# Three stages on one core: the dense stage's first steps dealt out anew over the last attention periods, and later transfers regrouped

## The chip, the cores and the metric

One core of a Trainium2 chip runs the whole program. The metric is the device time in microseconds (us) of one execution. Engines by the names of the profile: PE is TensorE (matmuls and transposes), DVE is VectorE, ACT is ScalarE, POOL is GpSimd, SP is SyncE, which issues nearly all transfers (SPq is its sequencer).

## The reference

Talking-heads attention with B = 4, 12 heads, 448 positions, 64 values a head; then a dense layer 768 to 2048 to 768 with ELU; then a mixture of 8 experts, each token going to its best one, with a skip.

```python
scores = scale * q @ k.T
scores = einsum('bhij,hg->bgij', scores, w_pre)
attn = softmax(scores)
attn = einsum('bhij,hg->bgij', attn, w_post)
x = (attn @ v)                       # 1792 tokens of 768
h = x @ w_in                         # w_in, w_out come as float64
x = where(h > 0, h, exp(min(h, 0)) - 1) @ w_out
do_compute = x @ w_skip > 0
e_idx = argmax(xc @ w_gate)          # of the tokens with do_compute
h = maximum(xc[mask] @ w1[e], 0)     # for each expert e
out = x;  out[do_compute] = xc + prob * (h @ w2[e])
```

## The kernel before, in words

**Attention.** The queries are cut into 16 tiles (4 per batch, 120, 120, 120 and 88 queries), each into 3 units: NP = 48 periods. Period n runs the softmax of unit n and the second mixing and value product of units before it, and the scores of a tile five periods ahead. `relayout` (line 189) copies a unit's scores from the tile s into the eight buffers d by DMA, in a layout in which heads and queries share partitions (d<-s on SP, line 197); `mix_pre` (L205) multiplies them by the first mixing matrix, `top` (L213, DVE) takes the maxima, `softmax` (L226, ACT) the exponentials with their sums, `mix_post` (L265) the second mixing; its results are copied to `at` (L271, ACT and DVE) and `av` (L286, L293) multiplies them with v; DVE copies the product to x (L302, L305), and SP stores it to xT (L313). Each unit has two halves; the copies d of unit n + 1's second half and of unit n + 2's first half are issued in period n.

**Dense layer.** `mixtures` is a generator called mix; each `next(mix)` runs it to its next yield. In the last five periods (n = 43 to 47, the flag `late`) four steps are woven into each: after the softmax, after the copies, after the second `mix_post` and at the period's end. Two more follow while attention ends. The steps load a weight chunk f of float64 (L518), narrow it to float32 on the chip (L529 on ACT; L532, L534, L537 and L539 on DVE; L541 on POOL; a generator with steps of its own), and load blocks of tokens xr from xT (`load_x`, L552). `high_x` (L556, ACT) and `low_x` (L560, DVE) split each into a high and a low half, as is done for weights (`split`, L504 and L505), and a product is made of three matmuls (high x high, high x low, low x high). products(s) (L626) makes 18 matmuls for one weight chunk and one block of 448 tokens; `elu` (L633, L634, L636) follows. `w_jobs` narrows the following chunks. `tables` (L589 and around) loads the gate's weights wgt and transposes them. The order of everything up to `order.close()`, in `mixtures` behind `tables`, is the order of the code, because `manual_schedule` is open; from there a scheduler orders the instructions of each engine.

**Second dense product, routing and experts.** The second product (L899) goes over 14 tiles of 128 tokens. Its weights w_out are partly in memory already; seven narrowed chunks wf are loaded again (wr, L845) through the pool raw0 of three buffers. `route` and `seat` find a token's expert and place. The experts' stage gathers the tokens of each expert with an indirect DMA on POOL (xg, L1072), transposes them (pt, L1082), and multiplies by w1 (L1094) and w2 (L1107), whose low halves DVE makes (wlo, L1067). After the first two experts `plan` orders the rest, and `reorder` (L1030 to L1038) makes the index list `ordered` with six DVE operations, which the fourth gather needs.

All of SP's transfers go out in the order of its row; a transfer waits for the one eight before it.

Of the kernel before, what the change touches and what calls it, by code (L numbers as in the profile page):

```python
# [20 lines left out]
NK = DM // 128  # L21
# [57 lines left out]
def attention(tc, q, k, v, w_pre, w_post, xT, mix):  # L79
# [12 lines left out]
    with ExitStack() as ctx, ExitStack() as mixing, ExitStack() as scoring:  # L92
# [137 lines left out]
        def softmax(U):  # L230
            for e in exps(U):
                e()
# [160 lines left out]
        for n in range(NP):  # L393
# [34 lines left out]
            for U in cur[1:]:  # L428
                softmax(U)
            if late:  # L430
                next(mix)
            for m in moves:
                m[1](nc.scalar.copy)
                m[0](nc.vector.tensor_copy)
            keys = T1 < len(tiles) and tiles[T1][1] == 0
# [31 lines left out]
        moves[0]()  # L467
        moves.append(av(len(tiles) - 1, 2))
        for f in moves[1:]:
            f()  # L470
        store()
# [4 lines left out]
def mixtures(tc, order, xT, w_in, w_out, w_skip, w_gate, w1, w2, ident, gT, wf, wg, x2d, slots, out):  # L476
# [5 lines left out]
    with ExitStack() as top:  # L482
# [27 lines left out]
        with ExitStack() as ctx:  # L510
# [57 lines left out]
            def load_w_in(fc):  # L568
                return load_w(w_in[fc])
# [4 lines left out]
            def tables():  # L574
# [8 lines left out]
                nc.sync.dma_start(out=wgt[:, :, :E], in_=w_gate.rearrange("(k p) e -> p k e", p=128))  # L583
                nc.sync.dma_start(out=wgt[:, :, E], in_=w_skip.rearrange("(k p) -> p k", p=128))
# [59 lines left out]
            yield  # L644
            yield
# [3 lines left out]
            load_x(0)  # L649
            yield  # L650
            next(step)
# [5 lines left out]
            yield  # L657
            high_x(0, 0)
            yield
            low_x(0, 0)  # L660
            w = wi[0] = ring_a.tile([128, 2, DM], FP32R, tag="w", name="w")
            nc.scalar.copy(out=w[:, 0], in_=narrowed[0])
            yield
            nc.vector.tensor_tensor(out=w[:, 1], in0=narrowed.pop(0), in1=w[:, 0], op=ALU.subtract)
            high_x(0, 1)
            yield
            raws[1] = load_w_in(1)
            yield
            low_x(0, 1)
# [3 lines left out]
            high_x(0, 3)  # L673
            yield
            low_x(0, 3)
            yield
            load_x(1, range(4))
            yield
            high_x(0, 4)
# [22 lines left out]
            yield  # L702

# [5 lines left out]
            products(1)  # L709
            split_x(2, range(6))  # L710
            elu(1)
            load_x(3)
            products(2)
# [31 lines left out]
        with ExitStack() as ctx:  # L745
# [47 lines left out]
            def route(i, lg):  # L793
# [3 lines left out]
                nc.vector.max_index(out=ix, in_max=mx, in_values=lg[:, :E])  # L797
                nmx = st_p.tile([128, 1], FP32, tag="nmx", name="nmx")
# [6 lines left out]
                ef = st_p.tile([128, 1], FP32, tag="ef", name="ef")  # L805
                nc.vector.tensor_copy(out=ef, in_=ix[:, 0:1])
                do = st_p.tile([128, 1], FP32, tag="do", name="do")
                nc.vector.tensor_scalar(out=do, in0=lg[:, E:E + 1], scalar1=0.0, scalar2=None, op0=ALU.is_gt)
                oh = st_p.tile([128, E], FP32, tag="oh", name="oh")
                nc.vector.tensor_scalar(out=oh, in0=iota8, scalar1=ef, scalar2=do, op0=ALU.is_equal, op1=ALU.mult)  # L810
# [32 lines left out]
            for fc in range(EARLY, NF):  # L843
                raw = raw0.tile([128, 2 * DM], FP32, tag="w", name="wr")[:, :DM]
                last_wr = nc.sync.dma_start(out=raw, in_=wf[fc - EARLY])  # L845
                wo[fc] = split(raw, ring_a if fc < RA + RB else ring2)
# [41 lines left out]
            for i, n, fc, cs in work:  # L888
# [35 lines left out]
                if fc == NF - 1:  # L924
                    if 0 in cs:
                        x2 = rows[i] = x2_p.tile([128, DM], FP32, tag="x2", name="x2")
                    for c in cs:
                        to, at = x2[:, cols[c]], po[c][:, :cols[c].stop - cols[c].start]
                        nc.scalar.copy(out=to, in_=at)  # L929
                        if last and c == 1:  # L930
                            turned, freed = score_turned(x2, c)
                            place_old(range(2))
                            logits(turned)
                            place_old(range(2, 5))
# [5 lines left out]
            place_old(range(5, NK))  # L940
# [9 lines left out]
        with ExitStack() as ctx:  # L950
# [289 lines left out]
            expert_first([0], [h], jobs(((3, 2), turn_h, h, ht, 0)))  # L1240
            expert_second(0, ht, jobs(((0,), turn_h, h, ht, 1), ((2,), turn_x, 1)))
            h = new_h()
            expert_first([1], [h], jobs(((1, 2), turn_x, 2)))
            reorder()
            xg[3] = gather(ids[3])
# [111 lines left out]
```

## Time and profile before

| what | us |
|---|---|
| median of three runs | 1022.62 |
| their range | 1020.44 to 1026.99 |
| the profiled execution's own time | 1024.68 |
| its span, first to last instruction | 1022.9 |
| attention, to the end of its last value product | 0 to 362.38 |
| the woven periods, n = 43 to 47 | 311.49 to 348.66 |
| first dense product | 362.38 to 596.46 |
| second dense product and routing | 596.46 to 848.91 |
| experts' products | 848.91 to 1015 |

The profile is one execution. Its table of stretches gives each engine's busy time in a stretch, and the granted clock of TensorE as a share of full speed: 0.50 is 1.2 GHz, 1.00 is 2.4 GHz. The list of waits gives, for a line of one engine, what ended its idle time, the sum, the count and the longest. In the timelines a row starts with its start and its length; "<-" in the brackets names what ended the idle time ahead of the row.

### The profile page before, as it was taken

How to read it: one execution, taken by the hardware profiler on the slowest of the kernel's cores; microseconds unless marked ns; L12 is line 12 of the kernel's file. 1: busy time of each engine (PE TensorE's matmuls, PEld its weight loads, DVE VectorE, ACT ScalarE, POOL GpSimd, SP SyncE). 2: the span in 40 equal slices, each digit the busy share in tenths (PEclk: the TensorE clock that was granted, in tenths of full speed). 3: DMA queues.
4: the chain of work that ended last, by engine and by line, in shares of the span. 5: the costliest groups of instructions: out<-in, count | busy, mean ns of one | idle time of the engine just before them, and what ended most of it. 6: DMA issues, size and time to landing. Idle time of an engine off the chain costs nothing. (4 is left out here: it accounts for less than half of the span.)

```text
span 1022.9 us, 30007 instructions
## 1 busy us (share of the span) xinstructions
PE 982.5 (96%) x12226; PEld 860.5 (84%) x12226; DVE 725.8 (71%) x1458; ACT 555.9 (54%) x1121; POOL 226.8 (22%) x295
## 2 busy tenths in 40 slices
PE   7899999999998899999999999999999999899997
PEld 4577777777766788999999999999999988799987
DVE  5677776777765777666666477777777748999963
ACT  5687787788765654445444462222222116788851
POOL 2233224224223312232332200010101003321002
PEclk9999999999998989999999999999999999999999
DMA  4665665675646565454665489543434396999800
GB/s 157 214 206 158 218 208 149 205 235 131 216 167 204 160 220 166 156 183 151 227 220 192 140 281 301 155 124 93 123 95 123 99 344 237 393 396 398 322 9 34
DMA packets 132297, 199.67 MB, mean 195 GB/s; under 512 B 35476, under 2 KB 99480, under 8 KB 131901
## 3 DMA queue, kind: packets, MB, share of 16 engines
q1 hardware_dynamic: 130013, 191.27, 56.4%
q0 software_dynamic: 2144, 6.46, 1.6%
q8 instruction: 97, 1.59, 0.7%
q14 instruction: 43, 0.35, 0.1%
HBM read 122.47 MB, written 37.65 MB: 157 GB/s over the span
## 5 line engine op out<-in xcount | busy, mean ns | idle before, releaser
L899 PE MATMUL o<-w,gh 128*128 128x384 f32 (+2 forms) x1344 | 239.2, 337 | 1.2 <-DVE w L505 0.8
L899 PEld LDWEIGHTS o<-w,gh 128*128 128x128 f32 x1344 | 231.9, 188 | 4.5 <-DVE w L505 1.4
L626 PE MATMUL h<-xh,w 128*128 128x448 f32 x1152 | 235.4, 367 | 0.0
L626 PEld LDWEIGHTS h<-xh,w 128*128 128x128 f32 x1152 | 217.4, 189 | 17.3 <-issue 0.4
L265 PEld LDWEIGHTS f<-kr,e 64*64 64x64 f32 x5888 | 106.3, 136 | 39.1 <-issue 29.5
L213 DVE TENSOR_REDUCE nmx<-c 128x1 f32<-128x448 f32 x184 | 102.4, 617 | 51.7 <-PE c L205 51.6
L226 ACT ACTIVATE e<-c,nmx 128x448 f32<-128x448 f32 x184 | 114.2, 632 | 23.0 <-DVE nmx L213 22.8
L789 DVE SCALAR_TENSOR_TENSOR junk<-x,wrow 128x768 f32<-128x768 f32 x117 | 111.8, 955 | 18.3 <-ACT x L929 12.8
L246 POOL TENSOR_SCALAR kr<-kpost,rs 128x60 f32<-128x60 f32 x184 | 78.4, 448 | 200.1 <-DVE rs L241 110.2
L1067 DVE TENSOR_TENSOR wlo<-w1t,whi 128x1536 fp32r<-128x1536 f32 x64 | 111.0, 1751 | 14.3 <-ACT whi L1065 14.0
L265 PE MATMUL f<-kr,e 64*64 64x60 f32 (+1 forms) x5888 | 108.4, 219 | 7.3 <-issue 3.5
L541 POOL TENSOR_TENSOR wf<-a,p 128x768 f32<-128x768 f32 x32 | 66.6, 2081 | 187.2 <-DVE p L539 139.5
L1065 ACT CAST whi<-w1t 128x1536 fp32r<-128x1536 f32 x64 | 93.9, 1482 | 20.6 <-PE ph L1094 9.4
L164 PE MATMUL qk<-k,qq 64*120 64x448 f32 (+1 forms) x576 | 82.6, 408 | 8.1 <-ACT k L135 4.5
L774 ACT CAST gh<-gr 128x512 fp32r<-128x512 f32 x56 | 35.0, 624 | 98.7 <-PE o L899 39.1
L205 PE MATMUL c<-d,kpre_low 64*64 64x448 f32 x368 | 83.3, 554 | 3.0 <-ACT s L168 2.8
L205 PE MATMUL c<-d,kpre_up 60*64 60x448 f32 x368 | 81.8, 554 | 0.0
L271 ACT COPY at<-f 128x420 f32<-128x420 f32 (+1 forms) x136 | 65.4, 516 | 28.2 <-PE f L265 27.2
L164 PEld LDWEIGHTS qk<-k,qq 64*120 64x120 f32 (+1 forms) x576 | 52.1, 186 | 27.8 <-issue 4.6
L286 PE MATMUL xp<-at,v 128*64 128x120 f32 (+1 forms) x1152 | 67.5, 266 | 7.3 <-issue 3.9
L168 ACT ACTIVATE s<-qk 120x448 f32<-120x448 f32 (+1 forms) x96 | 51.7, 544 | 35.5 <-PE qk L164 26.4
L169 DVE TENSOR_SCALAR s<-qk 120x448 f32<-120x448 f32 (+1 forms) x96 | 58.3, 621 | 16.1 <-PE qk L164 8.4
(180 smaller groups left out, 1255.7 us busy)
## 6 DMA issues: line engine op xcount, KB each, us to landing
w1t<-in_moe_w_dram SPq DMA_DIRECT2D x64, 768.0 KB
d<-s SPq DMA_DIRECT2D x176, 210.0 KB
gT<-g SPq DMA_DIRECT2D x64, 224.0 KB
f<-in_moe_w_in_dram SPq DMA_DIRECT2D x16, 768.0 KB
f<-in_moe_w_out_dram SPq DMA_DIRECT2D x16, 768.0 KB
gr<-gT SPq DMA_DIRECT2D x48, 256.0 KB
rk<-in_k_dram SPq DMA_DIRECT2D x24, 224.0 KB
v<-in_v_dram SPq DMA_DIRECT2D x24, 224.0 KB
```

The lines of the kernel that those rows point to most:

```text
L164: nc.tensor.matmul(out=ps[:n, :S], lhsT=qt[T, p // 2][rows, a, p % 2, :n], rhs=kt[b, p][rows, z, :], start=(i == 0), stop=(i == 2))
L205: nc.tensor.matmul(out=ps[j * UP:(j + 1) * UP, :S], lhsT=kpre_up[UP:UP + HP, :] if z else kpre_low, rhs=d[z, j])
L213: nc.vector.tensor_reduce(out=t, in_=c, op=ALU.max, axis=AX.X, negate=True)
L226: nc.scalar.activation(out=e, in_=c, func=ACTF.Exp, bias=t, accum_out=sms[0][:, k + i:k + i + 1])
L246: nc.gpsimd.tensor_scalar(out=kr, in0=kposts[z], scalar1=rs[:, 2 * i + z:2 * i + z + 1], scalar2=None, op0=ALU.mult)
L265: nc.tensor.matmul(out=ps[to, heads, z, :], lhsT=e[rows, keys * JW:(keys + 1) * JW], rhs=kr[rows, first * HR:(first + n) * HR])
L286: nc.tensor.matmul(out=ps[i][z * 64:(z + 1) * 64, :n], lhsT=vt[b, p][:, jc * 2 + z, :], rhs=att[T][:, jc * H + ORDER.index(2 * p + z), :n] ...
L626: nc.tensor.matmul(out=ps, lhsT=w[:, a, kk, :], rhs=xs[tb, kk][:, z, :], start=(kk == 0 and a + z == 0), stop=(kk == NK - 1 and a == 1))
L789: nc.vector.scalar_tensor_tensor(out=t[:, o:o + n], in0=x2, scalar=1.0, in1=w, op0=ALU.mult, op1=ALU.mult, accum_out=lg[:, e:e + 1])
L899: mm = nc.tensor.matmul(out=po[c][:, :cols[c].stop - cols[c].start], lhsT=gs[i][fc // GC][:, a, fc % GC, :], rhs=wo[fc][:, z, cols[c]], st ...
L1065: nc.scalar.copy(out=hi, in_=t)
L1067: nc.vector.tensor_tensor(out=lo, in0=t, in1=hi, op=ALU.subtract)
```

## The change

It does six things. (A) In late periods the copies to `at` of the first `mix_post` now stand ahead of the second half's softmax, and the first woven step behind both. The steps themselves are dealt out anew: the first token block is loaded in three pieces (2, 2, 2) and from one step before the narrowing on; the narrowing begins one step later; chunk 1 and the second block's loads come at other steps. (B) products(1) moves to a step of its own between the second and third value product of attention's end. (C) The loads of wgt move from `tables` to just behind the loads of the fourth token block. (D) Two chunks wf share one buffer of raw0. (E) `reorder` and the fourth gather move ahead of the first expert's second product. (F) In `route` three small operations move ahead of the exponential; in the last tile one block of `place_old` moves to a place after the last route.

```diff
-            for U in cur[1:]:
-                softmax(U)
-            if late:
-                next(mix)
+            if not late:
+                for U in cur[1:]:
+                    softmax(U)
             for m in moves:
                 m[1](nc.scalar.copy)
                 m[0](nc.vector.tensor_copy)
+            if late:
+                for U in cur[1:]:
+                    softmax(U)
+                next(mix)
...
         moves = [av(len(tiles) - 1, 0), av(len(tiles) - 1, 1, [ps_f.tile([128, 512], FP32, tag="f", name="xp") for _ in range(2)])]
-        moves[0]()
-        moves.append(av(len(tiles) - 1, 2))
-        for f in moves[1:]:
+        for f in moves:
             f()
+        next(mix)
+        av(len(tiles) - 1, 2)()
         store()
...
-                nc.sync.dma_start(out=wgt[:, :, :E], in_=w_gate.rearrange("(k p) e -> p k e", p=128))
-                nc.sync.dma_start(out=wgt[:, :, E], in_=w_skip.rearrange("(k p) -> p k", p=128))
...
             raws[0] = load_w_in(0)
             yield
             yield
+            load_x(0, range(2))
+            yield
+            yield
+            load_x(0, range(2, 4))
             yield
             step = narrowing(raws.pop(0))
             next(step)
             yield
-            load_x(0)
-            yield
             next(step)
             yield
+            load_x(0, range(4, 6))
+            yield
+            high_x(0, 0)
+            yield
             next(step)
             yield
             narrowed[0] = next(step)
             yield
-            yield
-            high_x(0, 0)
+            raws[1] = load_w_in(1)
             yield
...
-            load_x(1, range(4))
-            yield
-            high_x(0, 4)
             yield
             low_x(0, 4)
...
             elu(0)
             wi[1] = split(narrowed.pop(1), ring_a)
             yield
+            products(1)
+            yield
...
             raws["out"] = load_w_out(0)
-            products(1)
             split_x(2, range(6))
             elu(1)
             load_x(3)
+            nc.sync.dma_start(out=wgt[:, :, :E], in_=w_gate.rearrange("(k p) e -> p k e", p=128))
+            nc.sync.dma_start(out=wgt[:, :, E], in_=w_skip.rearrange("(k p) -> p k", p=128))
             products(2)
...
-            for fc in range(EARLY, NF):
-                raw = raw0.tile([128, 2 * DM], FP32, tag="w", name="wr")[:, :DM]
-                last_wr = nc.sync.dma_start(out=raw, in_=wf[fc - EARLY])
-                wo[fc] = split(raw, ring_a if fc < RA + RB else ring2)
+            for f0 in range(EARLY, NF, 2):
+                raw = raw0.tile([128, 2, DM], FP32, tag="w", name="wr")
+                fcs = range(f0, min(f0 + 2, NF))
+                for fc in fcs:
+                    last_wr = nc.sync.dma_start(out=raw[:, fc - f0], in_=wf[fc - EARLY])
+                for fc in fcs:
+                    wo[fc] = split(raw[:, fc - f0], ring_a if fc < RA + RB else ring2)
...
-                            place_old(range(2, 5))
+                            place_old(range(2, 4))
...
-            place_old(range(5, NK))
+            place_old(range(4, NK))
...
             expert_first([0], [h], jobs(((3, 2), turn_h, h, ht, 0)))
+            reorder()
+            xg[3] = gather(ids[3])
             expert_second(0, ht, jobs(((0,), turn_h, h, ht, 1), ((2,), turn_x, 1)))
             h = new_h()
             expert_first([1], [h], jobs(((1, 2), turn_x, 2)))
-            reorder()
-            xg[3] = gather(ids[3])
```

ACT's row in the woven periods n = 43 to 45: at is the copy behind the second mixing, e an exponential with its sum, a the narrowing's first step on the weight chunk f. Before:

```order
L271 COPY at<-f 128x42x10 x2
L226 ACTIVATE e,sm<-c,nmx 128x448 x4
L271 COPY at<-f 128x42x10 x3
L529 ACTIVATE a<-f_7170 128x768
L226 ACTIVATE e,sm<-c,nmx 128x448 x4
L271 COPY at<-f 128x42x10 x3
```

and now:

```order
L271 COPY at<-f 128x42x10 x2
L226 ACTIVATE e,sm<-c,nmx 128x448 x2
L271 COPY at<-f 128x42x10
L226 ACTIVATE e,sm<-c,nmx 128x448 x2
L532 ACTIVATE a<-f_7172 128x768
L271 COPY at<-f 128x42x10 x2
```

The step on f stood ahead of period 44's exponentials and now stands behind them; a copy to at stands between the two pairs.

SP's row in the same periods: f is the weight chunk, d<-s a half unit's scores (two rows for each half), xT a stored value product, xr a load of 128 x 448 tokens. Before:

```order
L518 DMA f_7170<-in_moe_w_in_dram 128x1536
L197 DMA d_154<-s 120x1x448
L197 DMA d_155<-s 120x1x448
L313 DMA xT_60<-x 128x2x120
L197 DMA d_156<-s 120x1x448
L197 DMA d_157<-s 120x1x448
L552 DMA xr<-xT_57 128x448 x6
L197 DMA d_158<-s 120x1x448
L197 DMA d_159<-s 120x1x448
```

and now:

```order
L521 DMA f_7172<-in_moe_w_in_dram 128x1536
L555 DMA xr<-xT_57 128x448 x2
L197 DMA d_154<-s 120x1x448
L197 DMA d_155<-s 120x1x448
L313 DMA xT_60<-x 128x2x120
L197 DMA d_156<-s 120x1x448
L197 DMA d_157<-s 120x1x448
L555 DMA xr<-xT_57 128x448 x4
L197 DMA d_158<-s 120x1x448
L197 DMA d_159<-s 120x1x448
```

Two of the six loads xr moved ahead of the second half of unit 45 (d_154, d_155); the other four stay between unit 46's first half and its second.

PE's row at the end of attention: xp are the value products (three pieces of the last tile), h the products of the first dense layer, 18 matmuls for each products(s). Before:

```order
L286 MATMUL xp<-at,v 64x88 x12
L293 MATMUL xp<-at,v 64x88 x4
L286 MATMUL xp<-at,v 64x88 x12
L293 MATMUL xp<-at,v 64x88 x4
L626 MATMUL h<-xh,w 128x448 x175
L589 MATMUL pt<-ident,wgt 8x128 x6
```

and now:

```order
L627 MATMUL h<-xh,w 128x448 x18
L286 MATMUL xp<-at,v 64x88 x12
L293 MATMUL xp<-at,v 64x88 x4
L627 MATMUL h<-xh,w 128x448 x108
L590 MATMUL pt<-ident,wgt 8x128 x6
```

products(1) stands ahead of the third value product, and the transposes of wgt come after 108 more matmuls instead of 175.

## Rows read from the trace of the kernel before

**Rows 1.** The page's busy time of TensorE, its share and instructions.

```profile
PE 982.5 (96%) x12226; PEld 860.5 (84%) x12226; DVE 725.8 (71%) x1458; ACT 555.9 (54%) x1121; POOL 226.8 (22%) x295
```

**Rows 2.** Stretches: length, busy time of each engine, clock, DMA share, GB/s.

```profile
317.32:328.12 10.80, 6.59 (x188) 5.16 (x181) 5.69 (x12) 4.80 (x12) 2.06 (x5) 0.85 0.83 259
328.12:335.15 7.03, 7.03 (x192) 5.48 (x187) 4.28 (x10) 5.09 (x13) 4.02 (x6) 0.75 0.51 145
335.15:341.01 5.86, 5.33 (x186) 4.22 (x181) 5.58 (x13) 5.40 (x15) 2.75 (x5) 1.00 0.53 167
...
357.01:362.38 5.37, 2.46 (x33) 2.07 (x32) 2.99 (x7) 4.38 (x9) 0.00 (x0) 0.69 0.93 288
...
402.35:596.46 194.11, 194.11 (x963) 180.17 (x960) 124.50 (x180) 92.59 (x152) 53.26 (x26) 1.00 0.54 182
...
848.91:886.72 37.81, 37.55 (x191) 32.33 (x190) 37.54 (x71) 29.90 (x32) 15.46 (x11) 1.00 0.92 337
...
889.73:1015.00 125.27, 125.27 (x685) 115.67 (x686) 100.04 (x88) 83.03 (x82) 19.46 (x11) 1.00 0.66 253
```

**Rows 3.** TensorE's waits: line, releaser, us in total, times, longest.

```profile
PE pt L1082 <- DMA xg<-x2d,ordered: 3.0, 1, 3.0
PE xp L286 <- DVE x L302: 2.9, 1, 2.9
...
PE pt L589 <- DMA wgt<-in_moe_w_gate_dram: 2.2, 1, 2.2
PE f L265 <- DVE at L271: 2.1, 1, 2.1
...
PE o L899 <- DVE w L505: 0.8, 2, 0.4
...
PE o L899 <- ACT w L504: 0.4, 2, 0.2
```

**Rows 4.** Timelines of ACT and VectorE in period 44.

```profile
321.44 0.89 ACT L529 ACTIVATE a<-f 128x768 f32<-128x768 f32 x1 [2.92 <-issue]
...
322.36 0.56 DVE L532 TENSOR_SCALAR a<-a 128x768 int32<-128x768 int32 x1 [5.72 <-ACT a L529]
```

**Rows 5.** SP's timeline from 314; then transfers of 312 to 332, 40 slices.

```profile
314.46 1.67 SPq L518 DMA_DIRECT2D f<-in_moe_w_in_dram  x1
...
321.83 4.30 SPq L552 DMA_DIRECT2D xr<-xT  x6
326.23 1.71 SPq L197 DMA_DIRECT2D d<-s  x2
...
DMA  7120556549798885866666788699989988779653
...
DMA packets 2838, 4.31 MB, mean 216 GB/s; under 512 B 957, under 2 KB 2707, under 8 KB 2835
```

**Rows 6.** VectorE's and ACT's timelines around the end of attention.

```profile
354.56 3.30 DVE L560 TENSOR_TENSOR xh<-xr,xh 128x448 fp32r<-128x448 f32 x6 [0.51 <-ACT xh L556]
...
359.53 0.33 DVE L302 COPY x<-xp 128x176 f32<-128x176 f32 x1
...
371.55 0.55 ACT L633 ACTIVATE m<-h 128x448 f32<-128x448 f32 x1 [1.70 <-PE h L626]
...
382.21 2.81 DVE L560 TENSOR_TENSOR xh<-xr,xh 128x448 fp32r<-128x448 f32 x3
```

**Rows 7.** The second load of wgt on SP, and its reader on TensorE.

```profile
398.82 0.57 SPq L584 DMA_DIRECT2D wgt<-in_moe_w_skip_dram  x1
...
401.78 0.82 PE L589 MATMUL pt<-ident,wgt 128*8 128x128 f32 x6 [2.19 <-DMA wgt<-in_moe_w_gate_dram]
```

**Rows 8.** ACT's timeline at the loads of stored chunks.

```profile
609.58 1.78 ACT L504 CAST w<-wr 128x768 fp32r<-128x768 f32 x2 [1.87 <-DMA wr<-wf]
```

**Rows 9.** The fourth gather on POOL, and a copy of VectorE ahead of it.

```profile
881.48 2.25 POOL L1072 DMA_INDIRECT xg<-x2d,ordered  x1 [6.36 <-DVE ordered L1035]
...
868.19 0.54 DVE L1084 TENSOR_TENSOR xt<-pt,xt 128x384 fp32r<-128x384 f32 x1
```

More of the change, by code (lines that the diff above doesn't have):

```diff
@@ L648, in mixtures @@
             yield
-            load_x(0)
+            next(step)
             yield
-            next(step)
+            load_x(0, range(4, 6))
+            yield
+            high_x(0, 0)
             yield
@@ L656, in mixtures @@
             yield
-            yield
-            high_x(0, 0)
+            raws[1] = load_w_in(1)
             yield
             low_x(0, 0)
+            high_x(0, 1)
+            yield
             w = wi[0] = ring_a.tile([128, 2, DM], FP32R, tag="w", name="w")
             nc.scalar.copy(out=w[:, 0], in_=narrowed[0])
+            low_x(0, 1)
             yield
             nc.vector.tensor_tensor(out=w[:, 1], in0=narrowed.pop(0), in1=w[:, 0], op=ALU.subtract)
-            high_x(0, 1)
-            yield
-            raws[1] = load_w_in(1)
-            yield
-            low_x(0, 1)
             high_x(0, 2)
@@ L673, in mixtures @@
             high_x(0, 3)
+            load_x(1, range(2))
+            yield
+            high_x(0, 4)
+            load_x(1, range(2, 4))
             yield
             low_x(0, 3)
-            yield
-            load_x(1, range(4))
-            yield
-            high_x(0, 4)
             yield
@@ L702, in mixtures @@
             yield
+            products(1)
+            yield
             ring_b = pool("ring_b", RB)
@@ L797, in route @@
                 nc.vector.max_index(out=ix, in_max=mx, in_values=lg[:, :E])
+                ef = st_p.tile([128, 1], FP32, tag="ef", name="ef")
+                nc.vector.tensor_copy(out=ef, in_=ix[:, 0:1])
+                do = st_p.tile([128, 1], FP32, tag="do", name="do")
+                nc.vector.tensor_scalar(out=do, in0=lg[:, E:E + 1], scalar1=0.0, scalar2=None, op0=ALU.is_gt)
+                oh = st_p.tile([128, E], FP32, tag="oh", name="oh")
+                nc.vector.tensor_scalar(out=oh, in0=iota8, scalar1=ef, scalar2=do, op0=ALU.is_equal, op1=ALU.mult)
                 nmx = st_p.tile([128, 1], FP32, tag="nmx", name="nmx")
@@ L804, in route @@
                 nc.vector.reciprocal(out=pairs[:, i, 1:2].bitcast(FP32), in_=sm)
[L805 to L810, printed above, removed]
                 return i, oh, do
```

## The prediction

> **What bounds the kernel now.** I read the busy table first: TensorE is busy 982.5 us, 96% of the span [rows 1], so the most that any reordering can take out is the other 40 us, and only where TensorE's own waits, or a lower clock, get shorter. Then the table by stage [rows 2], in which the granted clock is the third figure from the end. Two stretches stand out. The woven periods: the one from 317.32 (n = 44 of 0 to 47) takes 10.80 us for 6.59 us of TensorE work, and the next takes 7.03, all of it busy but at a granted clock of 0.75 (the mean of a stretch at half clock, 1.2 GHz, and one at full, 2.4 GHz); the one after them, 335.15 to 341.01, takes 5.86 at full clock for the same kind of work. And the end of attention, 357.01 to 362.38: 2.46 us busy in 5.37, clock 0.69. After 362.38 TensorE is nearly full, with three waits left. Third the list of TensorE's waits [rows 3], which gives each of these its releaser. The reader is to see there that six rows, 11.4 us, name a thing that the diff moves. Last the timelines of the engines that release them [rows 4 to 9]. Idle time of the others I don't count: it costs nothing unless it ends in one of the rows of TensorE.
>
> The profiled execution took 1024.68 us around its span of 1022.9; the median of three runs is 1022.62, 2.06 lower. The sum is made against 1024.68 and its difference is taken off the median.
>
> **A. The woven periods.** What is wrong in period 44 is ACT's place in a row. Its narrowing step (line 529) stands ahead of the exponentials and waits for the weight chunk f, issued on SP at 314.46 [rows 5] and used at 321.44, with 2.92 idle ahead of it; VectorE's shift (line 532) waits 5.72 behind that, and the maxima of the softmax are queued behind the shift [rows 4]. TensorE then waits 2.1 for `at` of VectorE [rows 3] and the clock falls: 10.80 + 7.03 for two periods that take 5.86 each undisturbed. In the changed kernel the step stands a place later, behind the exponentials, where ACT arrives after f has landed. No instruction is added. If nothing else came up the gain would be 17.83 - 11.72 = 6.1 us, and that is the upper end.
>
> Against it stands SP's queue. The loads xr, six of 224 KB, were issued 321.83 to 326.13 [rows 5], behind most of the copies d<-s that the next periods read. Now two stand ahead of period 45's last d, and all six ahead of period 46's. From f to the second d of period 46 that is f 768 KB, six xr 1344, six d 630 (105 each), one xT 120: 2862 KB, 2.93 MB. At the mean 216 GB/s of this stretch [rows 5] it needs 13.6 us; the transfers' share is at 9 tenths from 316.5 on [rows 5], where f follows two d's, so I let it begin at 316.8; the last of it then moves at 330.4. A transfer needs some time until its reader goes: the gate weights' load was issued by 399.39 and read at 401.78 [rows 7], 2.4 us with its own transfer, so I take half, 1.2: period 46 can begin at about 331.6. Before, it began at 335.15, so 3.55 is gained; undisturbed periods would begin it at 317.32 + 11.7 = 329.0, so 2.6 of the 6.1 is not. ACT gets the weight's cast and two more casts in period 46 (its 5.40 of 5.86 [rows 2] becomes over 6), 0.6 lost. **Taken 3.0**, from 0 (d later still) to 6.1. The 13.6 us count all that was issued ahead of the last d; that f, the only transfer ahead in its own row, was in use 6.98 us after its issue [rows 4, 5] doesn't show whether a small copy may pass large loads. The Trainium skill, "DMA: Bandwidth & Descriptors", section "Queues, rings and completion order", says that on each DMA engine the descriptors of one ring are consumed in order, and that SP owns one ring on each. By that rule d can't pass, and the sum is the one below; were it otherwise, the six xr would be no hindrance, A would be 6.1 - 0.6 = 5.5, and the sum 14.6.
>
> **B. products(1) between the last two value products.** Before, the third value product waits 2.91 for VectorE's copy of x at 359.53 [rows 3, 6], which is queued behind six subtractions, ELU's last step and a weight's subtraction; the clock is 0.69 there [rows 2]. Now 18 matmuls that wait for nothing (their low halves are the six subtractions from 354.56 on, 0.55 each against three matmuls of 0.6 [rows 6]) fill it: 963 matmuls take 194.11 us [rows 2], 0.2016 each, so 18 take 3.6, more than the wait of 2.9. The value product follows from 357.01 + 3.6 = 360.6, with 1.4 of its own at full clock, to 362.1. ACT's first step of ELU on products(2) stood at 371.55 [rows 6], so products(2) ended about 371.5. Now products(2) begins when the first low half of the third token block is there, which waits for the copy behind the value product: about 0.9 later, 363.0, and ends 366.6. That is 4.9 sooner. Not all stays: the low halves of the fourth block (VectorE 382.21, three in 2.81 [rows 6]) are behind a chain of VectorE work that starts only some 3 us sooner, and products(6), four blocks of 3.6 behind 363.0, reaches them at about 379.3 against 379.7 plus what the next ones lag: 1.3 to 1.4 given back. **Taken 3.5**, from 2 (the clock falls once more) to 5.
>
> **C. The gate's weights loaded earlier.** Two transfers of SP are moved from behind products(7) to behind the loads of the fourth token block, ahead of products(2): six blocks of 3.6 us sooner. The transposes waited 2.19 for them [rows 3, 7]; nothing else in the row waits, and the loads are small. Two issues (0.57 for the one at 398.82 [rows 7]) now stand ahead of an f load there; its reader on ACT is several blocks away. **2.2**, from 1.5.
>
> **D. Two stored chunks of w_out in one buffer.** Three buffers now take six loads, so all seven begin without waiting for a buffer's reader. Before, ACT waited 1.87 for such a load at 609.58 [rows 8], and the second product waited 0.8 + 0.4 behind ACT and VectorE [rows 3]. **1.2**, from 0: the tokens' chunks gr for the next tile now stand behind the large loads of wrow on SP. Their cover is the rest of the first tile's products, and no row says whether it is enough.
>
> **E. The experts' reordering before the second product.** The gather of `ordered` waited on POOL 6.36 for VectorE and went out at 881.48 [rows 9]; TensorE's transposes then waited 3.02, the stretch 886.72 to 889.73 being empty, [rows 2, 3]. Now the six small operations of VectorE stand ahead of the first expert's second product, between the low halves of ht, and the gather goes out near 862, six us ahead of xt at 868.19. Its price: VectorE is busy 37.54 of 37.81 us there [rows 2], so what moves ahead delays what TensorE reads next, as xt at 868.19 [rows 9]: about eight small operations of 0.15 ahead of it, 0.6 behind the present margin. After 889.73 TensorE is 100% busy to 1015 [rows 2], so a gain there passes on to the end. 3.0 - 0.6 and something for the weights' low halves, which have the same margin: **taken 2.2**, from 1 to 3.
>
> **F. route() and place_old.** Some VectorE operations of 0.15 us change places and one block of transposes is taken later; TensorE is not waiting there in any row of rows 3. **0**, up to 0.5.
>
> The sum: 3.0 + 3.5 + 2.2 + 1.2 + 2.2 = 12.1, 1024.68 - 12.1 = 1012.6 by the execution, 1022.62 - 12.1 = **1010.5** by the median.
>
> **The rivals.** *All of A and B.* The copies d<-s arrive in time and the fourth block gives nothing back: 6.1 + 5 + 2.2 + 1.2 + 2.2 = 16.7, 1005.9. For it: d is read only one or two periods after its issue. Against: the 13.6 us above, which leave period 46 without margin.
>
> *The queue eats A.* The d's of periods 45 and 46 land after all that stands ahead of them, at 216 GB/s and with SP waiting for each eighth transfer before (the six xr took 4.30 to issue). Period 46 begins where it did, A is 0, and the clock falls in the tail as before, so B is 2: 0 + 2 + 2.2 + 1 + 1.5 = 6.7, 1015.9. For it: f itself needed from 314.46 to 321.44, 6.98 us for 768 KB behind two d's.
>
> *The gaps come back elsewhere.* TensorE gains what it then waits for at the next place, all parts within 3 us: 1019.6 to 1025.6. For it: VectorE is at 99% in the experts [rows 2]. Against: the 194.11 us of products with no gap have VectorE at 124.5.
>
> *Slower.* The d's of periods 45, 46 and 47 each land so late that TensorE waits as VectorE did behind f, 5.7, and the clock halves each time; the drop in periods 44 and 45 made their busy time 6.59 + 7.03 instead of twice 5.33 [rows 2], 3.0 more. That is 3 x 8.7 = 26.1 lost against the 9.1 of B to E: +17.0, 1039.6. It decides once more than 3.0 us is lost in each of the three; against it, only 448 KB more, 2.1 us, is put ahead of period 45's d.
>
> **Chances.** Forecast 0.45 (1007.5 to 1013.5), all of A and B 0.17 (1003 to 1007.5), the queue 0.27 (1013.5 to 1018), gaps come back 0.06, slower 0.05. 1% is 10.2 us, about what a measurement of this kernel can tell from no change; 1012.4 is the bound, which cuts the forecast's range at 0.34 against 0.11. So faster 0.34 + 0.17 = 0.51, same 0.11 + 0.27 + 0.06 = 0.44, slower 0.05. The range 1004 to 1018 leaves out 0.06 + 0.05 and the outer 0.05 of two cases.
>
> **What would show it.** In the profile after: periods 44 and 45 near 5.9 each with clock 1.00, ACT's narrowing without idle ahead of it (A); if instead mix_pre's matmuls (line 205) wait for d, the queue has eaten it. No wait for x of line 302, products(1) of 3.6 at full clock ahead of the last value product, and a new short wait for xh at line 627 (B). No wait for wgt, wr or xg among TensorE's waits (C, D, E), and VectorE still at 99% from 849 to 887. Wrong is the sum if a clock drop stays in either stretch, or if a new row over 2 us stands in the waits of TensorE in dense2's second tile or at xt.

## The result, and the profile after

The changed kernel took 1010.22 us (median of 4 runs, 1009.65 to 1014.86) against 1023.41 for the kernel before (4 runs): a ratio of 0.9863 with a 95% interval of 0.982 to 0.9905. In a second comparison, with five more rounds, the ratio was 0.9899 (0.9869 to 0.9929), medians 1011.99 and 1022.68. The prediction was 1010.5. By the second interval the gain is 7 to 13 us of 1022.7.

The profiled execution has a span of 1008.7 us against 1022.9. TensorE's waits after, to be held against [rows 3] (line, releaser, us in total, times, longest; a line of after is 0 to 10 above its number before):

```profile
PE xp L286 <- issue: 3.6, 3, 2.6
PE h L627 <- DVE xh L563: 2.9, 2, 2.3
```

and two rows of before that [rows 3] does not show:

```profile
PE xp L286 <- issue: 3.9, 3, 1.7
...
PE f L265 <- ACT at L271: 1.5, 3, 0.5
```

All six rows of [rows 3] are gone: x of line 302, wgt, xg, `at` of VectorE, and the two on w. So is the wait for `at` of ACT, 1.5. One row is new, the low halves xh with 2.9. The wait of the value products for nothing that the profile shows ("issue") is a little smaller in total, 3.6 after 3.9, but its longest is 2.6 after 1.7. The stretches that answer to [rows 2] (length; busy time of each engine; clock, DMA share, GB/s at the end): periods 44, 45 and 46, the tail with products(1), products(2) to (6), and the rest of the early dense stage.

```profile
314.76:323.99 9.23, 6.60 (x193) 5.51 (x188) 5.39 (x12) 4.80 (x12) 3.29 (x8) 0.83 0.84 246
323.99:330.85 6.86, 6.86 (x188) 4.66 (x184) 3.89 (x10) 4.48 (x12) 0.00 (x0) 0.73 0.74 218
330.85:336.32 5.47, 5.27 (x191) 4.08 (x184) 4.99 (x9) 4.64 (x13) 4.20 (x5) 1.00 0.61 160
...
352.15:357.67 5.52, 5.52 (x60) 4.67 (x58) 3.40 (x8) 5.46 (x12) 0.00 (x0) 1.00 0.92 279
357.67:377.70 20.03, 17.14 (x86) 15.31 (x83) 16.24 (x25) 11.24 (x20) 4.29 (x2) 1.00 0.79 242
377.70:385.21 7.51, 7.51 (x32) 6.66 (x33) 5.89 (x9) 1.58 (x4) 1.84 (x1) 0.77 0.28 77
```

The tail is full at clock 1.00, where it had 2.46 us busy in 5.37 at 0.69. But periods 44 and 45 still have the clock at 0.83 and 0.73 and take 9.23 and 6.86 us, not the 5.9 that the prediction named as the sign of A, and a new stretch at 0.77 stands behind 377.70.

To say where the time went I count matmuls. Both kernels issue the same number of each kind, so the start of the k-th matmul of a kind marks the same place in every trace, and the difference of two starts is a stretch. Each row below is worked out in that way from the starts of TensorE's rows; "h1" is the first product matmul of products(0), "h301" the 301st of that kind, "o49" the 49th of w_out's product, and the first row starts in period 43 with the 337th of the matmuls on d's lower half (kpre_low). Twelve further profiles, told below, are already in it, because a single pair of executions misleads, as will be seen.

| stretch | before, two profiles | changed, first profile | changed, others with that code |
|---|---|---|---|
| period 43 to h1 (A) | 36.39, 38.58 | 33.76 | 33.61 to 35.76, mean of seven with the first 34.60 |
| h1 to h301 (B, C) | 75.51, 74.00 | 72.63 | 69.22, 69.31, 69.47, 69.51, 69.71, 72.53 |
| h301 to o49 | 180.65, 180.65 | 180.65 | 181.86 to 182.19 (five), 180.65 (the one with 72.53) |
| o49 to o97 (D) | 10.61, 10.25 | 8.36 | 8.36, once 8.56 |
| w_out's last to the experts' first (F) | 8.93, 7.53 | 7.17 | 7.16 to 7.17 (four), 8.76 to 8.80 (six, clock fallen) |
| experts' first to their 73rd (E) | 49.18, 50.50 | 46.49 | 46.10 to 46.38, once 47.39 |
| the start to period 43, not changed | 312.27, 308.25 | 310.45 | 307.58 to 314.45 |

The last row is a warning: the part that no edit touches differs by up to 7 us between executions. The clock is not the whole of it: the shortest, 307.58, has the clock at half for 6.8 us, and the changed kernel's first, 310.45, not at all; TensorE's idle time there runs from 12.0 to 16.6 us. The profiled pair's 14.2 us of difference holds 1.8 of that.

### The profile page after: what moved, and what is told of

It is laid out like the page before. It is cut to its first block, busy times and chain, and to the rows that moved or that the text cites. A ratio compares the mean times of both kernels' runs of the same rounds, so it can differ in the third digit from the quotient of the medians.

```text
span 1008.7 us, 30010 instructions
## 1 busy us (share of the span) xinstructions
PE 978.7 (97%) x12226; PEld 857.4 (85%) x12226; DVE 724.2 (72%) x1458; ACT 556.3 (55%) x1121; POOL 241.6 (24%) x295
## 5 line engine op out<-in xcount | busy, mean ns | idle before, releaser
L1077 DVE TENSOR_TENSOR wlo<-w1t,whi 128x1536 fp32r<-128x1536 f32 x64 | 111.1, 1753 | 14.6 <-ACT whi L1075 14.2
```

The costliest lines, as they stand in the source:

```text
L1077: nc.vector.tensor_tensor(out=lo, in0=t, in1=hi, op=ALU.subtract)
```

## The experiments

**The wgt loads back.** Reading the two first profiles, the new wait of 2.31 at products(6) stood behind VectorE's ELU step for products(4), which waited for a store. VectorE of the changed kernel:

```profile
376.49 0.62 DVE L637 SCALAR_TENSOR_TENSOR g<-m,h 128x448 f32<-128x448 f32 x1 [2.75 <-DMA gT<-g]
```

The low halves are queued behind it. Ahead of that store SP now issues wgt, in small pieces.

```diff
-            nc.sync.dma_start(out=wgt[:, :, :E], ...)      # behind load_x(3)
-            nc.sync.dma_start(out=wgt[:, :, E], ...)
+                nc.sync.dma_start(out=wgt[:, :, :E], ...)  # in tables()
+                nc.sync.dma_start(out=wgt[:, :, E], ...)
```

> The changed kernel with the two loads of wgt back in tables(). Measure M: from the first matmul of products(0) to the 301st matmul of line 627's kind; 75.51 us before, 72.63 after. In the changed kernel VectorE's last ELU step for products(4) waits 2.75 us for a store of gT, the low halves behind it are late, and TensorE waits 2.31 with a drop of the clock behind it. Theory 1: the many small pieces of wgt, ahead of that store in SP's queue, make it late. Then the wait of 2.31 falls under 1 and the drop goes, while the wait for wgt of 2.2 returns: M about 72. Theory 2: the queue is full there with the loads of x and f alone, because products(1) was moved; then the 2.31 stays and the wait for wgt comes on top: M about 75.

M, from h1 to h301, was 70.80. TensorE's timeline:

```profile
358.82 16.66 PE L629 MATMUL h<-xh,w 128*128 128x448 f32 x81 [0.59 <-DVE xh L563]
376.24 16.43 PE L629 MATMUL h<-xh,w 128*128 128x448 f32 x80 [0.76 <-DVE xh L563]
393.82 0.82 PE L592 MATMUL pt<-ident,wgt 128*8 128x128 f32 x6 [1.16 <-DMA wgt<-in_moe_w_gate_dram]
```

The wait at products(6) was 0.76 and the clock did not fall. It looked like theory 1, and it wasn't, as the later runs show: with the loads where the change puts them, five other executions had M of 69.2 to 69.7. Nor was the store on time here: with wgt out of its way VectorE's ELU step for products(4) still waited 1.63 for it, against 0.7 to 1.3 in four of those five and nothing in the fifth. What the run does show is C: with wgt back, h1 to h301 is 1.4 longer than theirs (69.4), and the 1.16 of wait has returned. And the stretch behind was 180.65 here and about 182.1 there, so by o49 the run is level with them: 251.45 against 251.35 to 251.70.

**products(1) back.**

```diff
-        for f in moves:
+        moves[0]()
+        moves.append(av(len(tiles) - 1, 2))
+        for f in moves[1:]:
             f()
-        next(mix)
-        av(len(tiles) - 1, 2)()
...
             raws["out"] = load_w_out(0)
+            products(1)
```

> The changed kernel with products(1) back behind the third value product. Theory of the prediction: the idle 2.91 and the lower clock return and M (72.63 after) grows by the 3.5 us that B was to bring, to 76.1. Theory from the traces: B's gain of 4.6 is given back at products(6) by a wait for low halves and by a drop of the clock; without B that wait goes too, and M is within 0.8 of 72.9.

M was 71.97, h301 to o49 180.77. The wait of 2.91 was back as in [rows 3]:

```profile
PE xp L286 <- DVE x L302: 2.9, 1, 2.9
```

Against 69.4 the part is worth 2.5 at h301; at o49 it is worth 252.75 - 251.47 = 1.3 (251.47 is the mean of the five). Neither theory had it: the gain is less than 3.5, but it is not all given back at products(6).

**Three buffers for ELU's results.**

```diff
-            gs_p = pool("gs", 2, ctx, side="right")
+            gs_p = pool("gs", 3, ctx, side="right")
```

> The changed kernel with three instead of two buffers for ELU's results (pool gs), so that VectorE's step for products(4) need not wait for the store of products(2)'s. If that store is what makes the low halves late, the wait of 2.31 at products(6) falls under 0.6 and no drop of the clock follows: M from 72.63 to about 69. Rival: the low halves wait for the loads of x or for VectorE's own row, and M stays within 0.7 of 72.6.

M was 68.73. TensorE's row through products(6), without a wait:

```profile
361.48 22.16 PE L627 MATMUL h<-xh,w 128*128 128x448 f32 x107 [0.59 <-DVE xh L563]
```

With a buffer more, VectorE doesn't wait for the store, and TensorE doesn't wait for the low halves. The same in the last experiment below (68.63). Against the usual 69.4 it gains 0.7. The long wait of the first profile goes with a late store: VectorE waited 2.75 for it there, and 2.94 in the one other execution with such a wait. The store is not all of the short one: in two runs below, wgt behind products(5) and the loads of x later, VectorE's step does not wait for it, and TensorE still waits 0.5 for the low halves.

**wgt behind products(5)'s ELU.**

```diff
             elu(5)
+            nc.sync.dma_start(out=wgt[:, :, :E], ...)
+            nc.sync.dma_start(out=wgt[:, :, E], ...)
             products(6)
```

> The changed kernel with the two loads of wgt behind the ELU of products(5), so neither ahead of the store of products(2) nor as late as in tables(). Theory 1 of the first run (small pieces of wgt make the store late): the 2.31 falls under 1, no wait for wgt: M about 69.5. Theory 2 (the queue is full without them): M within 0.7 of 72.6.

M was 69.26, as theory 1 had it. But so it is with the loads in the change's place, in five executions of seven. The run does not tell the two theories apart. VectorE does not wait for the store here, but neither does it in one run with the loads in the change's place, so no run shows that wgt's small pieces delay the store.

**D, E and F undone.** The three edits of the diff are reversed: one chunk wf for each buffer, `reorder` and its gather behind the second expert's first product, `route` and `place_old` as before.

```diff
-            for f0 in range(EARLY, NF, 2):
+            for fc in range(EARLY, NF):
...
-            reorder()
-            xg[3] = gather(ids[3])
             expert_second(0, ht, jobs(((0,), turn_h, h, ht, 1), ((2,), turn_x, 1)))
             h = new_h()
             expert_first([1], [h], jobs(((1, 2), turn_x, 2)))
+            reorder()
+            xg[3] = gather(ids[3])
```

> The changed kernel with the three late parts undone at once, each read in its own stretch. D (one stored chunk for each buffer): from the 49th matmul of w_out's product to its 97th 10.6 us as before, 8.36 in the changed kernel. F (route and place_old): from that product's last matmul to the experts' first; 8.93 before, 7.16 in the changed kernel, but 8.80 in the three runs of it that had a clock drop of 3.4 us there. If F is worth the 1.77, the undoing gives 8.9 with no drop of the clock; if it is the clock alone, 8.8 to 8.95 with a drop and 7.2 to 7.3 without. E (reorder and the gather): from the experts' first matmul to the 72nd of that kind 49.17 before and 46.49 in the changed kernel; undone 49.2.

The stretch of D took 10.21 and that of E 49.21, with the waits of both back:

```profile
PE pt L1089 <- DMA xg<-x2d,ordered: 3.0, 1, 3.0
PE o L906 <- DVE w L508: 0.6, 2, 0.4
```

The stretch of F took 7.53 without a drop of the clock; the second profile of before has 7.53 too, without one. So F is worth 7.53 - 7.16 = 0.4, and the rest of the first pair's 1.76 is the clock. The routing's stretch of before, of the changed kernel, and of the run with wgt back, which has F as changed:

```profile
839.98:848.91 8.93, 8.11 (x52) 7.36 (x50) 3.39 (x35) 3.23 (x8) 2.11 (x3) 0.81 0.48 181
...
830.40:837.56 7.16, 6.34 (x51) 5.64 (x49) 3.44 (x35) 3.23 (x8) 1.62 (x3) 1.00 0.59 226
...
828.64:837.44 8.80, 7.98 (x51) 7.29 (x49) 3.44 (x35) 3.23 (x8) 2.11 (x3) 0.81 0.50 190
```

The same code gives 7.16 at clock 1.00 and 8.80 at 0.81. Which of the two comes is a matter of the execution.

**The woven periods: copies back, steps back, loads later, loads sooner.** Four runs take part A apart. In the first the copies stand behind both softmaxes again:

```diff
-            if not late:
-                for U in cur[1:]:
-                    softmax(U)
+            for U in cur[1:]:
+                softmax(U)
+            if late:
+                next(mix)
             for m in moves:
```

> The changed kernel with the order of copies and second softmax in the late periods as before, the woven steps as changed. From the 337th matmul on d (period 43) to products(0): 36.4 before, 33.8 to 35.6 in four runs of the changed order. If the copies' place matters, waits of TensorE for ACT at line 271 of 0.5 in two or three periods return and the stretch is 1 to 1.5 longer than the changed kernel's mean of 34.6; if the steps alone matter, no change.

In the second the steps of mix are those of the kernel before:

```diff
-            load_x(0, range(2))
-            yield
-            yield
-            load_x(0, range(2, 4))
             yield
             step = narrowing(raws.pop(0))
             next(step)
             yield
+            load_x(0)
+            yield
...
```

> The changed kernel with the woven steps dealt as before (loads of x in one piece, narrowing a step sooner), copies and softmax as changed. The narrowing's first step then again waits for f on ACT, now behind the exponentials of period 44: if the copies' and softmax's place alone removed the wait of VectorE, the stretch stays at 34 to 35.5; if the steps did, it is 36 to 37, with VectorE's shift waiting some 3 to 5 us.

In the third the first two loads of x are issued with the next two:

```diff
-            load_x(0, range(2))
             yield
             yield
-            load_x(0, range(2, 4))
+            load_x(0, range(4))
```

> The changed kernel with the first two loads of x a period's part later, behind the copies d of period 44, so that f alone stands ahead of them. In the changed kernel TensorE's wait put down to issue in period 44 was 2.6 to 4.2 in three of four runs, with the instruction queue's 16 KB load 7 to 9 us behind the one before it instead of 4 to 5. If data in flight delays that load, fewer bytes there make it 1 to 2 as before (1.7) and the stretch about 33.5; if the instruction load is late whatever stands ahead, the wait stays over 2.5.

and in the fourth all six are issued where the first two were:

```diff
-            load_x(0, range(2))
+            load_x(0, range(6))
             yield
             yield
-            load_x(0, range(2, 4))
...
-            load_x(0, range(4, 6))
```

> The changed kernel with all six loads of the first token block right behind f, ahead of the copies d of periods 45 and 46: 896 KB more there, the suspected cost doubled and more. Stretch from period 43's first matmul on d to products(0): 33.6 to 35.6 in six runs of the changed order. If TensorE's instruction load is delayed by data in flight, or d by what is ahead of it in SP's queue, TensorE's waits for issue and for d grow by about 896 KB at 216 GB/s, 4 us, and the stretch is over 36. If neither, under 35.6.

The stretch was 34.04, 34.54, 32.89 and 33.46, all in or below the changed order's 33.61 to 35.76, and all below the 36.39 and 38.58 of before. What ends TensorE's waits there moves about. With the copies back, of line 265 and issue:

```profile
PE xp L286 <- issue: 2.8, 1, 2.8
PE f L265 <- ACT at L271: 1.8, 3, 0.8
```

With the steps back:

```profile
PE f L265 <- ACT at L271: 3.0, 1, 3.0
PE xp L286 <- issue: 2.0, 1, 2.0
```

and VectorE's shift waits as long as it did before:

```profile
321.89 0.56 DVE L535 TENSOR_SCALAR a<-a 128x768 int32<-128x768 int32 x1 [6.17 <-ACT a L532]
```

With all loads of x ahead of the copies d:

```profile
PE c L205 <- DMA d<-s: 3.0, 2, 2.4
PE xp L286 <- issue: 1.8, 1, 1.8
```

So the waits behind ACT's `at` return, 1.8 and 3.0, when either half is undone, but the stretch doesn't show it: as far as single runs with a spread of 2.2 can tell, either half alone takes most of what both take, and VectorE's wait behind ACT's narrowing, which the steps put back with 6.17, does not make the stretch long by itself. Both halves were not undone together, other than in the kernel before. With the loads ahead, mix_pre does wait for d, 3.0 in all; the 4 us that the expectation added did not come.

That wait is not peculiar to this run. The run with three buffers, which has part A as the change has it, shows it too:

```profile
PE c L205 <- DMA d<-s: 2.3, 2, 1.7
```

There "issue" took only 0.7, TensorE came sooner to the second half of period 46, and its two copies d, issued behind the other four loads of x, were not there yet. At the value product of period 44 "issue" was 1.7 to 4.2 in eleven of twelve profiles of the changed kernel and its variants, 0.7 in the other. It does not follow the loads of x: with all six ahead it is 1.8, and with none ahead 1.7 in one run and 3.2 in the last one below. The theory that their bytes delay the instructions that TensorE waits for there falls. What the wait ends with can be read from the traces: in all fourteen, TensorE goes on 1.2 to 1.6 us after a 16 KB load on the queue that the profile calls "instruction" has ended, and the later that load starts behind the one before it, the longer the wait as a rule (4.7 us with a wait of 0.7, 9.1 with 4.2). That these are TensorE's own instructions is likely and not shown, and why the load starts late stays open.

**The kernel before, again.**

> The kernel before, profiled a second time, to see how far its stretches differ from one execution to the next. The places without a drop of the clock in either profile should agree within 0.2 us; the woven stretch (36.39), the tail up to products(1) (13.72) and the last routing (8.93) held drops in the first. If those are the kernel's own, all three come again; if a drop is a matter of the execution, one or two of them are shorter by 1 to 2 us.

The untouched part took 308.25 instead of 312.27, the tail from h1 to the 19th product matmul 12.60 instead of 13.72, the routing 7.53, the woven stretch 38.58. The waits themselves are the kernel's own and all came again:

```profile
PE f L265 <- DVE at L271: 3.2, 1, 3.2
PE xp L286 <- DVE x L302: 2.9, 1, 2.9
...
PE pt L1082 <- DMA xg<-x2d,ordered: 2.8, 1, 2.8
...
PE pt L589 <- DMA wgt<-in_moe_w_gate_dram: 1.9, 1, 1.9
```

The drops of the clock are not: this profile has one in the woven periods as the first, none in the tail nor in the routing, and one each behind the waits for wgt and xg, where the first had none.

**The changed kernel, again.**

> The changed kernel again, against the kernel before in five rounds. By the runs so far the ratio is 0.986 to 0.989. In four runs with the same code at products(6) the stretch from the 109th to the 301st product matmul took 40.1 to 40.7, not the 43.60 of the first profile; if that one was an exception, this profile has about 40.4 and the stretch behind it 182, 1.3 longer than the 180.65 of the first.

The ratio was 0.9899. The stretch from the 109th to the 301st product was 40.41, and the one to o49 182.19, as expected. VectorE and TensorE at products(6):

```profile
378.96 0.62 DVE L637 SCALAR_TENSOR_TENSOR g<-m,h 128x448 f32<-128x448 f32 x1 [0.94 <-DMA gT<-g]
...
380.27 5.49 PE L627 MATMUL h<-xh,w 128*128 128x448 f32 x26 [0.66 <-DVE xh L563]
```

The wait for the store is there, but 0.94 instead of 2.75, and TensorE's is 0.66 without a drop behind it. The first profile, and the run with all loads of x ahead (43.50), have the long one; five executions with the same code there have a short one, 0.4 to 0.8.

What it then loses, 1.5 from h301 to o49, can be seen in two rows of TensorE and two of ACT in the same profile. TensorE's listed waits are 0.49 and 0.18; the rest is lost pace between the starts, as told for D below.

```profile
467.32 14.81 PE L627 MATMUL h<-xh,w 128*128 128x448 f32 x72 [0.49 <-DVE g L637]
482.32 7.95 PE L627 MATMUL h<-xh,w 128*128 128x448 f32 x38 [0.18 <-DVE g L637]
...
463.66 0.90 ACT L532 ACTIVATE a<-f 128x768 f32<-128x768 f32 x1 [4.47 <-POOL wf L544]
478.66 0.89 ACT L532 ACTIVATE a<-f 128x768 f32<-128x768 f32 x1 [4.18 <-POOL wf L544]
```

The narrowing of the weights, ACT to VectorE to POOL and back to ACT, which waits for POOL's last result, comes round every 15.0 us for a pair of chunks. TensorE's four blocks of that time are 72 matmuls of 0.2022, 14.6. So TensorE gains 0.4 on the chain with each pair, and once it is far enough ahead it waits for ELU's step on VectorE (g), which frees the product's PSUM buffer and stands in the row with the narrowing. In the kernel before, and in the first profile after, TensorE was late enough not to meet it; no wait stands there. A gain ahead of this place is kept only up to that limit: with h1 as the origin, o49 came at 251.35 to 251.70 in five executions. With three buffers for ELU the chain itself ran 0.8 sooner (114.57 behind h1 at the first of these ACT rows, 115.38 here), and o49 came at 250.86 and 250.78. With C undone it came at 251.45 without meeting the limit.

**Loads later and three buffers together.** The edits of the two experiments above in one kernel.

> The changed kernel with the first token block's loads behind the copies d of period 44 and with three buffers for ELU's results. If the two gains of the single runs (1 to 1.5 in the woven stretch, 0.5 at products(6)) add up, it is 1 to 2 us below the changed kernel of the same call, which five rounds may just tell apart; if later waits take them back, no difference.

Its median was 1009.1 us, ratio 0.9885 (0.9853 to 0.9918), beside 1011.99 for the changed kernel, measured with it. The intervals overlap; the trace gives 250.78 against 251.70 from h1 to o49 and 34.52 in the woven stretch, inside the changed kernel's own spread. So 0.6 to 0.9 us from the third buffer are shown, twice, by the trace, and nothing from the loads. It is the lowest median of the three kernels that were run more than once.

## Why the prediction was right, point by point

The total was right: 12.1 us predicted, 13.2 and 10.7 between medians. Part of that is luck. B and C together were taken 2.3 too large, D, E and F 2.0 too small, and A has its size by a working that is wrong. The prediction also named a sign of being wrong, a clock drop that stays in one of its two stretches, and that sign is there: the drop in the woven periods stayed, and the total came out even so.

**A, taken 3.0: right in size, by luck.** The mean of the seven is 34.60 against 36.39 and 38.58, 2.9 from the middle of the two. The prediction halved the 6.1 because the copies d behind the loads would hold back period 46. Its working has an error of size: it counts a copy d as 105 KB, and the profile of before lists twice that.

```profile
d<-s SPq DMA_DIRECT2D x8, 210.0 KB
```

With 210 the bytes are 3492 KB, the time at 216 GB/s is 16.6 us, period 46 begins at 334.6 instead of 335.15, and with the 0.6 for ACT nothing is left of A: the same working with the right size says 0, and a total of 9.1. The transfers themselves did take that long: in the seven profiles with the changed order the sixth d landed 17.9 to 19.2 us after f was issued, where the prediction's sum gives 15.9 and the one with 210 KB 18.9. But they were not what held TensorE back as a rule. In the first profile after, nothing waited for d, though the last one landed only 1.2 us before its reader started; d is waited for, 2.3 us, in the run with three buffers, where "issue" is short, 3.0 where all six loads stand ahead, and 0.4 in the run with products(1) back. What holds period 45 back is the wait of "issue" at the value product of period 44, and the lower clock behind it. It stood in the trace of before with 1.7, and the prediction didn't count it among the things that stay. The step named for it, VectorE's 5.72 behind ACT, did go: ACT's first narrowing step waits 0.28, VectorE's shift 2.19, and TensorE has no wait for VectorE in these periods. But the run with the steps back has that wait of VectorE again, 6.17, with a stretch of 34.54, so that it is not shown to be what cost the 2.9; which edit of A brought them stays open.

```profile
319.79 0.89 ACT L532 ACTIVATE a<-f 128x768 f32<-128x768 f32 x1 [0.28 <-issue]
320.71 0.56 DVE L535 TENSOR_SCALAR a<-a 128x768 int32<-128x768 int32 x1 [2.19 <-ACT a L532]
```

**B, taken 3.5, and C, taken 2.2: together 5.7, measured 3.4.** The places behaved as described. The first product of products(3) started 9.06 earlier than before in the first profile, of which 4.45 were there at h1: 4.6, predicted 4.9. The wait at products(2) was 0.59, predicted 0.9; that at products(6) 0.4 to 0.8 in five executions and 2.2 to 2.3 in two, predicted 1.3. (That 1.3 has no sum behind it: by the prediction's figures products(6) starts at 377.4, four blocks of 3.6 behind 363.0, and its 379.7 comes from no row.) By h301 the gain of both was 75.51 - 69.4 = 6.1 against the first profile of before, 4.6 against the second. What failed is the step "a gain there passes on", which the prediction wrote down for E alone and took for granted here: from h301 to o49 the products stood in [rows 2] with no gap in 194 us, VectorE busy 124.5 of them, and that was read as slack. It is slack of an engine, but the narrowing chain through three engines let only 4.7 us of the 6.1 through (256.16 - 251.47 from h1 to o49). It took 1.5 back. So the two parts overlap: on top of the other, B is worth 1.3 at o49 and C nothing, and each without the other takes more than that. Against the two profiles of before, o49 is 4.7 and 3.2 sooner with B and without C (251.45), 3.4 and 1.9 with C and without B (252.75), in one run each. The mean over the seven profiles, two of them with the long wait at products(6), is 252.0 from h1 to o49 against 255.4 before: 3.4.

**D, taken 1.2: measured 2.1.** The mechanism was right, the term too small. The listed waits were 1.17; the stretch lost 2.25, then 1.89, and 1.85 when undone. A wait in the list runs from the modelled end of a matmul to the next start. Matmuls start every 0.174 us there (8.36 for 48), but each is drawn with 0.34 us, so each of the four breaks hides another 0.17 of lost pace: 1.17 + 0.7 = 1.9. The loads of gr behind wrow, which the prediction kept as its lower end, cost nothing: the next tile took the same time.

**E, taken 2.2: measured 2.9 (2.7 to 3.1).** The gather goes out at 850.02 instead of 881.48, or 861.4 if the experts' first product is put at the same time as before, where the prediction said near 862. The wait of 3.02 is gone, and TensorE is full from 879.79 to 1001 as predicted. The price of VectorE's reordering, taken as 0.6 and more, was 0.3 to 0.4 in the first profile (46.49 beside the usual 46.1 to 46.2) and next to nothing in most others; in one, the run with the loads of x later, TensorE waited 1.1 for ht of VectorE, and the stretch was 47.39.

```profile
850.02 0.95 POOL L1082 DMA_INDIRECT xg<-x2d,ordered  x1 [3.17 <-DVE swapped L1046]
```

**F, taken 0, up to 0.5: measured 0.4** without a drop of the clock in either and 0.15 with one in both.

**The rivals.** All of A and B did not come. That the queue eats A did not come either, though its ground held: the copies d did not pass the loads. The rule of the Trainium skill, "DMA: Bandwidth & Descriptors", section "Queues, rings and completion order", that descriptors are consumed in ring order on each DMA engine, agrees with the landings in these traces. By the semaphores of the transfers there are 264 pairs around the woven periods of the fourteen profiles in which a d was issued with an earlier load f or xr still under way; d landed first in one of them. The section does not say that the transfers also complete in order, so the prediction's "d can't pass" goes a step beyond it; here the landings show it. "The gaps come back elsewhere" did in part, at a place that the rival didn't name.

The measured terms are 2.9 + 3.4 + 2.1 + 2.9 + 0.4 = 11.7.

## What to carry to other kernels

Count how far ahead of a bound engine the slowest chain of helpers is, over the stretch that follows, before crediting a gain: a long stretch with no wait shows that the chain keeps up at the present lead, not with a larger one. Sum short breaks of a matmul row by the starts, from the k-th matmul to the next, since the listed waits leave out the pace that is lost in each. Hold the size of a transfer in a sum against the list of transfers: here 105 KB for 210 gave a gain of 3.0 us where the same sum with 210 gives none. And compare two profiles of the same kernel before reading one pair: here a wait of 2.31 with a drop of the clock behind it, in the first profile after, came in two of seven executions and led to a theory that the first experiment seemed to confirm.

## What the runs showed that was not expected

The clock falls at different places in executions of the same code: the routing took 7.16 to 7.17 at clock 1.00 and 8.76 to 8.80 at 0.81. The untouched first 310 us differ by up to 7 us, by more than the clock. TensorE's wait for "issue" in period 44, 0.7 to 4.2 us in fourteen profiles, can be longer than any wait that the change removed there. It ends 1.2 to 1.6 us behind a 16 KB load on the instruction queue each time, and no run here found what makes that load late.
